# First pairs of a fused attention and gated unit: transposes without casts, attention outputs in single PSUM banks, and w_out exchanged by a permutation matmul

## The chip, the cores and the metric

The kernel runs on one core of one Trainium2 chip. Times are microseconds (us) of one execution on the device. A run that takes over 1.5% more than the fastest of the same kernel is marked slow; ratios use fast runs alone. The profile is one traced execution; its span is a little shorter than the run's time (183.2 us of span in an execution of 185.49 us of the kernel before). PE is TensorE (PEld its weight loads), DVE VectorE, ACT ScalarE, POOL GpSimd, SP SyncE. PEclk is the clock that PE was granted, as a share of full speed.

## The reference

Attention with a causal window, then a gated linear unit with a causal convolution of 5 taps. q, k and v are (8 batches, 8 heads, 576 positions, 64), in fp32. Heads 0 to 3 see the last 32 positions, heads 4 to 7 every fourth one of the last 128.

```python
scores = scale * np.matmul(q, k.transpose(0, 1, 3, 2))
mask_plain = (rel >= 0) & (rel < window)
mask_dil = (rel >= 0) & (rel < window * dilation) & (rel % dilation == 0)
...
x = attn_out.transpose(0, 2, 1, 3).reshape(B, S, H * D)      # (8, 576, 512)
for k in range(K):
    gate_pre += conv_w[k][None, None, :] * xp[:, k:k + S, :]
gate = 1.0 / (1.0 + np.exp(-gate_pre))
return gate * (x @ w_val) @ w_out
```

## The kernel before

Two heads make a pair; there are 32 pairs, numbered 0 to 31. Two pairs make a group, which is one load of q and k, and four pairs make a batch. Two of the four residues of the positions are held with their two heads exchanged, so they need w_val and w_out with the 64-row halves exchanged: `w_val_s` and `w_out_s`. The second was made by a copy from SBUF to SBUF through the DMA engines:

```python
def swap_out():
    for h in range(2):
        nc.gpsimd.dma_start(out=w_out_s[D * h:D * h + D], in_=w_out_b[D - D * h:2 * D - D * h])

def out_tile(G, n):                       # output projection of one half G
    w = w_out_b if G == 0 else w_out_s
    ps = bank()                           # one of 4 single PSUM banks
    ...                                   # 4 matmuls of 512 columns
    osb = out_pool.tile([128, Dm], FP32, name="osb")     # 4 buffers
    nc.scalar.mul(out=osb, in_=ps, mul=0.5)
    ...                                   # stores on the SP queue
```

The order of instructions is the program's own. The loop over pairs, cut to what the change touches:

```python
for i in range(NP):
    ...                                   # loads of groups ahead, on the SP queue
    if i + 1 < NP:
        prep_v(i + 1)                     # v to bf16, on POOL
    if i == 2: ...                        # casts of q, k of group 2, on POOL
    if i == 5:
        swap_out()
    scores(i, 0); scores(i, 1)            # PE, then exp on ACT
    run_conv(i - 1)
    apply_mask(i, 0)                      # DVE
    if i > 0: after_x(i - 1)              # transposes of pair i-1's result
    if 1 < i < NCH: next_pair(i)          # transposes of q, k of pair i+1
    apply_mask(i, 1)
    if 0 < i < 3: make_conv_diag(i + 1)   # DVE
    ...
    attn_v(i, 0); attn_v(i, 1)            # into the banks of the scores
    normalize(i)                          # DVE: one reciprocal, one multiply
    if i == 1 or NCH <= i < EARLY: next_pair(i)
    if i == EARLY - 1: trans_main(g + 1, "k")            # i = 6: group 4
    if i == 0: next_pair(0); finish_mask_d()
    elif i >= EARLY - 1 and a == 0 and g + 1 < 2 * B: trans_rest(g + 1)
    ...                                   # value matmuls, output projections
```

`trans_rest` transposes the last 64 rows of each head of a group, which come by transfers of their own ("rest rows", `qk_rest`).

The softmax here doesn't subtract the row's maximum and nothing guards it: scores larger than these inputs give would overflow.

## Time and profile before

| what | the kernel before |
| --- | --- |
| time, three runs | 184.03 us (183.78 to 184.43) |
| span of the profiled execution | 183.2 us |
| PE waiting for w_out_s | 5.2 us, once |
| pair 7, pair 8, pair 31 start | 44.0, 53.9, 160.7 us |
| PE at half clock | 9.6 to 16.4 and 50.5 to 57.4 us |

The profiled execution (185.49 us) was somewhat longer than these three. Two more are needed for the comparison. The first is the page's chain of the work that ended last, by engine; the second a stretch of the early pairs: its length, then busy us (and instructions) of PE, PEld, DVE, ACT and POOL, PEclk, DMA share and GB/s.

```profile
PE 72%; DVE 7%; POOL 6%; DMA 6%; issue 4%; ACT 2%; POOLq 0%; ACTq 0%
```

```profile
20.00:30.00 10.00, 7.75 (x154) 5.22 (x153) 7.00 (x16) 6.53 (x15) 4.61 (x7) 1.00 1.16 262
```

DMA holds 6% of the chain, and that is the one copy of w_out. In the early stretch no engine is full; only the DMA share is.

### The profile page before, as it was taken

To read this page: it belongs to the slowest core of one execution; us is meant where nothing else is said; L and a number is where in the kernel's file an instruction comes from. 1 tells how busy PE (TensorE), PEld (TensorE's weight loads), DVE (VectorE), ACT (ScalarE), POOL (GpSimd) and SP (SyncE) were. 2 spreads that over 40 slices of the span, in tenths; PEclk is the share of its full clock that TensorE was granted. 3 is DMA by queue.
4 is the path that set the end of the run, shared out by engine and by line. 5 is a ranking of instruction groups with operands and counts; after the bars stand their busy time and mean duration, and the time that the engine had idled before them with its cause. 6 is when DMAs were issued, how large, how long until landed. Compare 5 with 4: busy or idle time off the path is not lost.

```text
span 183.2 us, 6768 instructions
## 1 busy us (share of the span) xinstructions
PE 158.7 (87%) x2799; PEld 108.8 (59%) x2827; DVE 120.2 (66%) x292; ACT 115.9 (63%) x217; POOL 59.2 (32%) x118
## 2 busy tenths in 40 slices
PE   6768878979259999999996999999999999999990
PEld 2445556656137667667774776777677767665540
DVE  4647667855404988688775766976797869773320
ACT  3625764759227677777874788778877786564440
POOL 7857166065302730850093028300750400000000
PEclk9957999999957999999999999999999999999999
DMA  5999999999999999999999999999999322224354
GB/s 149 249 300 326 236 263 260 357 197 193 206 338 245 214 319 362 231 334 334 291 222 300 296 291 221 307 309 290 185 333 343 106 61 61 61 57 106 104 166 145
DMA packets 51688, 42.91 MB, mean 234 GB/s; under 512 B 6997, under 2 KB 46917, under 8 KB 51658
## 3 DMA queue, kind: packets, MB, share of 16 engines
q1 hardware_dynamic: 49888, 40.57, 84.1%
q0 software_dynamic: 1216, 1.57, 4.9%
q8 instruction: 22, 0.36, 0.9%
q10 hardware_dynamic: 554, 0.34, 0.6%
q14 instruction: 8, 0.07, 0.1%
HBM read 33.56 MB, written 9.44 MB: 235 GB/s over the span
## 4 chain that ended last, share of the span: by engine, by line
PE 72%; DVE 7%; POOL 6%; DMA 6%; issue 4%; ACT 2%; POOLq 0%; ACTq 0%
PE ps_bank L599 17%; PE ps_bank L583 14%; PE ps_bank L566 12%; PE ps_bank L365 7%; DMA w_out_s<-w_out_b 6%; PE ps_sc L479 5%; PE ps_sc L436 3%; PE ps_sc L493 3%; PE ps_sc L453 3%; DVE et L465 3%; PE ps_bank L520 3%; PE ps_bank L533 2%; DVE xn L508 2%; PE ps_bank L527 2%; DVE xT L535 1%
## 5 line engine op out<-in xcount | busy, mean ns | idle before, releaser
L456 ACT ACTIVATE et<-ps_sc 128x576 bf16<-128x576 f32 x64 | 38.5, 648 | 13.8 <-PE ps_sc L436 9.9
L604 ACT ACTIVATE osb<-ps_bank 128x512 f32<-128x512 f32 x36 | 21.9, 608 | 32.7 <-PE ps_bank L599 26.1
L589 DVE SCALAR_TENSOR_TENSOR y<-gate,ps_bank 128x288 bf16<-128x288 bf16 x64 | 28.3, 450 | 11.8 <-PE ps_bank L583 9.6
L508 DVE TENSOR_TENSOR xn<-ps_sc,rec 96x768 bf16<-96x768 f32 (+1 forms) x32 | 30.6, 955 | 1.1
L566 PE MATMUL ps_bank<-xT,conv_diag 64*64 64x288 bf16 (+1 forms) x768 | 27.9, 270 | 0.0
L193 POOL CAST k_b<-k_nat 128x512 bf16<-128x512 f32 x14 | 9.2, 679 | 53.9 <-DMA k_nat<-in_k_dram 18.5
L465 DVE TENSOR_TENSOR et<-et,mask_p 128x576 bf16<-128x576 bf16 x32 | 17.4, 547 | 10.8 <-ACT et L456 10.8
L575 ACT ACTIVATE gate<-ps_bank 128x288 bf16<-128x288 f32 x64 | 23.0, 422 | 2.0 <-PE ps_bank L566 1.7
L599 PE MATMUL ps_bank<-w_out_s,y 128*128 128x512 bf16 x59 | 18.4, 394 | 6.1 <-DMA w_out_s<-w_out_b 5.2
L599 PEld LDWEIGHTS <-y 128*128 128x128 bf16 x144 | 12.8, 99 | 17.3 <-issue 6.6
L566 PEld LDWEIGHTS <-conv_diag 64*64 64x64 bf16 x768 | 19.3, 108 | 3.0 <-DVE qB L420 1.0
L583 PE MATMUL ps_bank<-xT,w_val_s 128*128 128x288 bf16 x128 | 20.7, 285 | 0.0
L583 PE MATMUL ps_bank<-xT,w_val_b 128*128 128x288 bf16 x128 | 19.9, 286 | 0.4 <-DVE xT L535 0.4
L465 DVE TENSOR_TENSOR et<-et,mask_d 128x576 bf16<-128x576 bf16 x32 | 15.5, 486 | 6.6 <-ACT et L456 6.4
L535 DVE COPY xT<-ps_bank 128x576 bf16<-128x576 bf16 x32 | 14.6, 456 | 7.4 <-PE ps_bank L533 4.4
L200 POOL CAST vP<-vPst 128x768 bf16<-128x768 f32 x16 | 13.1, 841 | 18.5 <-DMA vPst<-in_v_dram 16.7
L599 PE MATMUL ps_bank<-w_out_b,y 128*128 128x512 bf16 x58 | 17.7, 379 | 0.7
L503 DVE RECIPROCAL rec<-ps_sc 96x12 f32<-96x12 f32 (+1 forms) x32 | 7.4, 231 | 13.8 <-PE ps_sc L479 11.1
L583 PEld LDWEIGHTS <-w_val_s 128*128 128x128 bf16 x128 | 12.1, 97 | 5.6
L479 PE MATMUL ps_sc<-vP,et 64*128 64x65 bf16 x384 | 10.2, 197 | 5.4 <-POOL vP L200 2.9
L479 PEld LDWEIGHTS <-et 64*128 64x128 bf16 x384 | 7.7, 98 | 12.0 <-issue 5.7
L583 PEld LDWEIGHTS <-w_val_b 128*128 128x128 bf16 x128 | 11.7, 98 | 3.6 <-issue 0.2
(93 smaller groups left out, 239.2 us busy)
## 6 DMA issues: line engine op xcount, KB each, us to landing
k_nat<-in_k_dram SPq DMA_DIRECT2D x12, 512.0 KB, 6.5
q_nat<-in_q_dram SPq DMA_DIRECT2D x12, 512.0 KB, 8.0
vPst<-in_v_dram SPq DMA_DIRECT2D x12, 384.0 KB, 8.4
v_st<-in_v_dram SPq DMA_DIRECT2D x6, 512.0 KB, 6.4
k_nat<-in_k_dram SPq DMA_DIRECT2D x8, 256.0 KB, 4.5
out_dram<-osb SPq DMA_DIRECT2D x8, 256.0 KB, 6.4
q_nat<-in_q_dram SPq DMA_DIRECT2D x7, 256.0 KB, 5.0
out_dram<-osb SPq DMA_DIRECT2D x8, 224.0 KB, 5.2
```

The costliest lines, as they stand in the source:

```text
L200: nc.gpsimd.tensor_copy(vPs[b % NVP][:, a:e, :, 0:D], vPst[b % NVP][:, a * NB // 2:e * NB // 2, :].rearrange("p (h u) (j d) -> p h (u j) d ...
L456: nc.scalar.activation(out=e3, in_=ps[:, :, 0:HB], func=AF.Exp, scale=scale)
L465: nc.vector.tensor_tensor(out=e3, in0=e3, in1=m, op=ALU.mult)
L479: nc.tensor.matmul(out=ps[:, z, x * AVS:x * AVS + D + 1], lhsT=et[D * z:D * z + D, h2, col:col + 128], rhs=vPs[b % NVP][D * z:D * z + D, a ...
L508: nc.vector.tensor_tensor(out=dst, in0=av[:, :, :, 0:D], in1=rec[0:R, :, :, None].to_broadcast([R, 2, 6, D]), op=ALU.mult)
L535: nc.vector.tensor_copy(xTs[b % NXT][:, c, :, 2:], pr)
L566: nc.tensor.matmul(out=pss[G][D * hp:D * hp + D, o * T:(o + n) * T], lhsT=conv_diag[D * h:D * h + D, c, K - 1 - m, :], rhs=xt[D * h:D * h ...
L575: nc.scalar.activation(out=gate, in_=pss[G][:, 0:HB], func=AF.Tanh, scale=0.5)
L583: nc.tensor.matmul(out=ps[:, 0:HB], lhsT=w[:, mc, c * 128:(c + 1) * 128], rhs=xt[:, mc, 2 * G:2 * G + 2, 2:], start=(mc == 0), stop=(mc == ...
L589: nc.vector.scalar_tensor_tensor(out=y_half[G][:, c, b * HB:(b + 1) * HB], in0=gates.pop((b, c, G)), scalar=1.0, in1=ps[:, 0:HB], op0=ALU. ...
L599: nc.tensor.matmul(out=ps, lhsT=y_half[G][:, c, 128 * n:128 * n + 128], rhs=w[:, c, :], start=(c == 0), stop=(c == NCH - 1),)
L604: nc.scalar.mul(out=osb, in_=ps, mul=0.5)
```

## The change

The intent has two parts. (a) `w_out_s` comes from a matmul with an identity whose halves are exchanged, so the copy goes. (b) The first pairs are to start faster: q and k of groups 0 and 2 are transposed without a cast first, the transposes of the next pair go ahead of the attention output, and this output gets single banks instead of the scores' banks, so that the next scores need not wait for it. Output projections start at pair 6. The core of the diff (cuts marked):

```diff
-    def swap_out():
-        for h in range(2):
-            nc.gpsimd.dma_start(out=w_out_s[D * h:D * h + D], in_=w_out_b[D - D * h:2 * D - D * h])
+    def swap_out(m, eng):
+        ps = bank()
+        nc.tensor.matmul(out=ps, lhsT=ident_x, rhs=w_out_b[:, m, :], start=True, stop=True)
+        if eng is nc.scalar:
+            nc.scalar.copy(out=w_out_s[:, m, :], in_=ps)
+        else:
+            eng.tensor_copy(w_out_s[:, m, :], ps)
 ... trans_main
-                if not dil:
+                if not dil and g < 4:
+                    for h in range(2):
+                        nc.tensor.transpose(
+                            out=ps[D * h:D * h + D, z, TM * m:TM * m + TM],
+                            in_=hi_bf16(t[name][:, 2 * z + h, D * m:D * m + D]), identity=ident)
+                    continue
+                elif not dil:
 ... attn_v
-        et, ps = st[(i, "et")], st[(i, 1)]
+        if i >= EARLY_AV:                                  # EARLY_AV = 5
+            ps = [st[(i, 1)][:, f, :] for f in range(2)]
+        else:
+            if hf == 0:
+                st[(i, "av")] = [bank(), bank()]
+            ps = st[(i, "av")]
 ... normalize, for i < 5
+        for f in range(2):
+            av = st[(i, "av")][f][0:R, 0:6 * AVS].rearrange("p (x e) -> p x e", x=6)
+            nc.vector.reciprocal(out=rec[0:R, f, :], in_=av[:, :, D])
+            nc.vector.tensor_tensor(...)
 ... the loop
-        if i == 5:
-            swap_out()
-        if 1 < i < NCH:
+        if i < NCH:
             next_pair(i)
-        if 0 < i < 3:
-            make_conv_diag(i + 1)
+        if 0 < i < NCH:
+            make_conv_diag(i - 1)
+        if i == 6:
+            swap_out(0, nc.scalar)
+            swap_out(1, nc.scalar)
         normalize(i)
+        if i == 6:
+            swap_out(2, nc.scalar)
+            swap_out(3, nc.vector)
-            if outs:
+            if outs and i > 5:
                 run_out()
```

The order of POOL's work (v, masks, casts) is rearranged too, and in each of the first pairs one of the dummy matmuls on the tile `junk` (`warm`) is dropped.

More of the change, by code (lines that the diff above doesn't have):

```diff
@@ L55 @@
     NP = B * NCH
+    EARLY_AV = 5
     consts = ctx.enter_context(tc.tile_pool(name="consts", bufs=1))
@@ L74 @@
     ident = consts.tile([128, 128], BF16, name="ident")
+    ident_x = consts.tile([128, 128], BF16, name="ident_x")
     perm = consts.tile([96, 96], BF16, name="perm")
@@ L142, in load_rest, with load_v_half @@
                             ap=[[2 * D, 2 * TR], [S * D, 4], [1, 2 * D]]))
+    def load_v_half(g, z, a, e, eng):
+        b, per = g // 2, NB // 2
+        first, dst = a * per, vPst[b % NVP]
+        if b == 0 and a == 0 and z == 0:
+            eng.dma_start(
+                out=dst[16:D, 0, :],
+                in_=v[0, 0, 0:96, :].rearrange("(p j) d -> p (j d)", j=2))
+            first = 1
+        eng.dma_start(
+            out=dst[D * z:D * z + D, first:e * per, :],
+            in_=bass.AP(
+                tensor=v.tensor,
+                offset=v.offset + (b * H * S + 192 * first + 96 * z - 32) * D,
+                ap=[[2 * D, D], [192 * D, e * per - first], [1, 2 * D]]))
     def load_v(g, a=0, e=4, eng=nc.sync):
@@ L147, in load_v @@
         if not dil:
-            per = NB // 2
-            dst = vPst[b % NVP]
             for z in range(2):
-                first = a * per
-                if b == 0 and a == 0 and z == 0:
-                    eng.dma_start(
-                        out=dst[16:D, 0, :],
-                        in_=v[0, 0, 0:96, :].rearrange("(p j) d -> p (j d)", j=2))
-                    first = 1
-                eng.dma_start(
-                    out=dst[D * z:D * z + D, first:e * per, :],
-                    in_=bass.AP(
-                        tensor=v.tensor,
-                        offset=v.offset + (b * H * S + 192 * first + 96 * z - 32) * D,
-                        ap=[[2 * D, D], [192 * D, e * per - first], [1, 2 * D]]))
+                load_v_half(g, z, a, e, eng)
         else:
@@ L181, in load_group, with cast @@
         load_v(g)
-    def cast(g, name, a, eng):
+    def cast(g, name):
         t = grp_tiles[g]
-        if name + "b" not in t:
-            t[name + "b"] = qb_pool.tile([128, DIL, 4, D], BF16, name=f"{name}_b")
-        dst = t[name + "b"][:, :, a:a + 2, :]
-        src = t[name][:, a:a + 2, :].rearrange("p h (r d) -> p r h d", r=DIL)
-        if eng is nc.scalar:
-            nc.scalar.copy(out=dst, in_=src)
-        else:
-            eng.tensor_copy(dst, src)
+        t[name + "b"] = qb_pool.tile([128, DIL, 4, D], BF16, name=f"{name}_b")
+        for a in (0, 2):
+            nc.gpsimd.tensor_copy(
+                t[name + "b"][:, :, a:a + 2, :],
+                t[name][:, a:a + 2, :].rearrange("p h (r d) -> p r h d", r=DIL))
     def prep_v(i):
@@ L246 @@
     nc.vector.tensor_tensor(out=ident_h, in0=ident[:, 0:D], in1=ident[:, D:2 * D], op=ALU.add)
+    for h in range(2):
+        nc.vector.tensor_copy(ident_x[:, D * h:D * h + D], ident[:, D - D * h:2 * D - D * h])
     nc.gpsimd.memset(ident5, 0.0)
@@ L360, in trans_main @@
             for m in range(4):
-                if not dil:
+                if not dil and g < 4:
+                    for h in range(2):
+                        nc.tensor.transpose(
[3 more added lines that the diff above has]
+                elif not dil:
                     src = t[name + "b"][:, m, 2 * z:2 * z + 2, :]
@@ L373, in trans_main @@
                 dst = t["qT"][:, z0:z1, :, 0:TM]
-                if g == 0:
+                if g <= 2 and len(pairs) == 1:
                     nc.vector.tensor_copy(dst, rt)
@@ L469, in attn_v @@
         b, c, dil, g, a = pair_info(i)
-        et, ps = st[(i, "et")], st[(i, 1)]
+        et = st[(i, "et")]
+        if i >= EARLY_AV:
[4 more added lines that the diff above has]
+            ps = st[(i, "av")]
         if not dil:
@@ L479, in attn_v @@
                             nc.tensor.matmul(
-                                out=ps[:, z, x * AVS:x * AVS + D + 1],
+                                out=ps[z][:, x * AVS:x * AVS + D + 1],
                                 lhsT=et[D * z:D * z + D, h2, col:col + 128],
@@ L493, in attn_v @@
                 nc.tensor.matmul(
-                    out=ps[:, hf, x * AVS:x * AVS + D + 1], lhsT=et[:, hf, col:col + 128],
+                    out=ps[hf][:, x * AVS:x * AVS + D + 1], lhsT=et[:, hf, col:col + 128],
                     rhs=rhs, start=True, stop=True)
@@ L500, in normalize @@
         xn = st[(i, "xn")] = xn_pool.tile([128, 2, 3, 2, D], BF16, name="xn")
-        av = st[(i, 1)][0:R, :, 0:6 * AVS].rearrange("p f (x e) -> p f x e", x=6)
         rec = rec_pool.tile([128, 2, 6], FP32, name="rec")
-        nc.vector.reciprocal(out=rec[0:R], in_=av[:, :, :, D])
         if dil:
@@ L507, in normalize @@
             dst = xn[0:R].rearrange("p z n h d -> p z (n h) d")
-        nc.vector.tensor_tensor(
-            out=dst, in0=av[:, :, :, 0:D],
-            in1=rec[0:R, :, :, None].to_broadcast([R, 2, 6, D]), op=ALU.mult)
+        if i >= EARLY_AV:
+            av = st[(i, 1)][0:R, :, 0:6 * AVS].rearrange("p f (x e) -> p f x e", x=6)
+            nc.vector.reciprocal(out=rec[0:R], in_=av[:, :, :, D])
+            nc.vector.tensor_tensor(
+                out=dst, in0=av[:, :, :, 0:D],
+                in1=rec[0:R, :, :, None].to_broadcast([R, 2, 6, D]), op=ALU.mult)
+            return
+        for f in range(2):
+            av = st[(i, "av")][f][0:R, 0:6 * AVS].rearrange("p (x e) -> p x e", x=6)
+            nc.vector.reciprocal(out=rec[0:R, f, :], in_=av[:, :, D])
+            nc.vector.tensor_tensor(
+                out=dst[:, f], in0=av[:, :, 0:D],
+                in1=rec[0:R, f, :, None].to_broadcast([R, 6, D]), op=ALU.mult)
     def trans_x(i):
@@ L661 @@
     warm(8)
-    cast(0, "k", 0, nc.vector)
-    cast(0, "q", 0, nc.scalar)
     next_pair(-1)
-    setup_conv_w()
-    make_conv_diag(0)
-    make_conv_diag(1)
-    make_mask_d()
-    make_perm()
-    prep_v(0)
     for i in range(NP):
@@ L683 @@
             load_group(g + 3)
-        if i + 1 < NP:
-            prep_v(i + 1)
-        if i == 1:
+        if i == 0:
+            prep_v(0)
+            make_mask_d()
+            prep_v(1)
+            make_perm()
+        elif i == 1:
+            prep_v(2)
             load_weight(w_val_b, moe_w_val)
-        if i == 2:
-            for name in ("k", "q"):
-                cast(2, name, 0, nc.gpsimd)
-        if i == 3:
+        elif i == 2:
+            prep_v(3)
+        elif i == 3:
             load_weight(w_out_b, moe_w_out)
-            for name in ("k", "q"):
-                cast(2, name, 2, nc.gpsimd)
-        if i == 4:
+            prep_v(4)
+        elif i == 4:
             swap_val()
-        if i == 5:
-            swap_out()
-        g2 = g + 2
-        if 2 < g2 < 2 * B and g2 % 2 == 0:
-            cast(g2, "k" if a == 0 else "q", 0, nc.gpsimd)
-            cast(g2, "k" if a == 0 else "q", 2, nc.gpsimd)
+            prep_v(5)
+            prep_v(6)
+        elif i == 5:
+            prep_v(7)
+            cast(4, "k")
+        elif i == 6:
+            cast(4, "q")
+        else:
+            if i < NP - 1:
+                prep_v(i + 1)
+            if g + 2 < 2 * B and g % 2 == 0:
+                cast(g + 2, "k" if a == 0 else "q")
         scores(i, 0)
@@ L705 @@
         if i == 0:
-            cast(0, "k", 2, nc.scalar)
-            cast(0, "q", 2, nc.scalar)
+            setup_conv_w()
         run_conv(i - 1)
@@ L716 @@
         apply_mask(i, 1)
-        if 0 < i < 3:
-            make_conv_diag(i + 1)
+        if 0 < i < NCH:
+            make_conv_diag(i - 1)
         if i < NCH:
-            warm(3 if i == 0 else 2)
+            warm(2 if i == 0 else 1)
         elif c == 0 and outs:
             run_out()
-        elif vals:
+        elif i > NCH and vals:
             run_val()
@@ L726 @@
         attn_v(i, 1)
+        if i == 6:
+            swap_out(0, nc.scalar)
+            swap_out(1, nc.scalar)
         normalize(i)
-        if i == 1 or NCH <= i < EARLY:
+        if i == 6:
+            swap_out(2, nc.scalar)
+            swap_out(3, nc.vector)
+        if i == 0:
+            finish_mask_d()
+        elif i == NCH - 1:
+            make_conv_diag(i)
+        if NCH <= i < EARLY:
             next_pair(i)
@@ L731 @@
             trans_main(g + 1, "k")
-        if i == 0:
-            next_pair(0)
-            finish_mask_d()
-        elif i >= EARLY - 1 and a == 0 and g + 1 < 2 * B:
+        elif i >= EARLY and a == 0 and g + 1 < 2 * B:
+            trans_rest(g + 1)
+        if i == EARLY - 1:
             trans_rest(g + 1)
         if i < NCH - 1:
-            warm(2)
+            warm(1)
         if c == 0 and vals:
```

## The prediction

> **What bounds the kernel now.** I read the page first, then the waits of TensorE (PE), then the chain of waits, the timeline of the first 60 us, and a table of windows. There are 32 pairs of heads, numbered 0 to 31; a group is two pairs (one load of q and k), and four pairs are one batch.
>
> The page: busy shares, then the span in 40 slices of 4.6 us.
>
> ```profile
> PE 158.7 (87%) x2799; PEld 108.8 (59%) x2827; DVE 120.2 (66%) x292; ACT 115.9 (63%) x217; POOL 59.2 (32%) x118
> ...
> PE   6768878979259999999996999999999999999990
> ...
> PEclk9957999999957999999999999999999999999999
> DMA  5999999999999999999999999999999322224354
> GB/s 149 249 300 326 236 263 260 357 197 193 206 338 245 214 319 362 231 334 334 291 222 300 296 291 221 307 309 290 185 333 343 106 61 61 61 57 106 104 166 145
> ```
>
> PE is the busy engine, at 9 tenths from slice 12 (55 us) on with one exception. Its holes are in slices 0 to 11, above all the "25" at 46 to 55 us. The DMA row is full from slice 1 to slice 30: the loads run without a pause until about 142 us. So two things can bound the first 55 us: PE, or the arrival of the loads.
>
> The waits of PE in the first 56 us (total, times, longest):
>
> ```profile
> PE ps_bank L599 <- DMA w_out_s<-w_out_b: 5.2, 1, 5.2
> PE ps_sc L479 <- POOL vP L200: 2.9, 1, 2.9
> ...
> PE ps_sc L493 <- POOL vA L205: 1.3, 1, 1.3
> ...
> PE ps_bank L400 <- DMA qk_rest<-in_q_dram: 0.4, 1, 0.4
> ```
>
> The first is the largest: the output projection of the exchanged half waits for w_out_s, an SBUF to SBUF copy. The second is pair 0 waiting for its v; the third is pair 6. The last is small, yet decides how I read the change, as said below.
>
> The chain of waits around the large one (start, length):
>
> ```profile
> 40.59 0.48 POOL w_out_s L346
> 41.06 10.91 DMA w_out_s<-w_out_b
> 52.11 0.58 PE ps_bank L599
> ```
>
> And the timeline of PE there:
>
> ```profile
> 42.48 0.23 PE L400 MATMUL ps_bank<-ident,qk_rest 128*128 128x128 bf16 x1 [0.39 <-DMA qk_rest<-in_q_dram]
> ...
> 43.99 0.28 PE L453 MATMUL ps_sc<-qA,kA 64*128 64x128 bf16 x4
> ...
> 46.69 0.22 PE L493 MATMUL ps_sc<-vB,et 128*128 128x65 bf16 x2
> ...
> 52.11 0.58 PE L599 MATMUL ps_bank<-w_out_s,y 128*128 128x512 bf16 x1 [5.19 <-DMA w_out_s<-w_out_b]
> ```
>
> Pair 7 starts at 43.99, its last attention matmul ends at 46.9, then PE stands until 52.1. At 42.48, the end of pair 6, PE waited for the transfer of the rest rows of group 4: there it had caught up with the loads. The windows (busy by engine, clock, DMA share, GB/s):
>
> ```profile
> 35.00:40.00 5.00, 3.93 (x63) 2.71 (x65) 3.97 (x9) 3.60 (x8) 1.81 (x3) 1.00 1.19 249
> 40.00:45.00 5.00, 4.21 (x73) 3.04 (x73) 2.33 (x7) 3.47 (x7) 3.65 (x8) 1.00 1.17 194
> 45.00:50.00 5.00, 1.91 (x38) 1.59 (x30) 2.85 (x6) 2.09 (x4) 1.60 (x2) 1.00 1.10 200
> 50.00:55.00 5.00, 2.67 (x41) 1.48 (x46) 0.00 (x0) 0.99 (x2) 0.00 (x0) 0.55 1.11 330
> ```
>
> The DMA share is over 1 all the time, and the clock is halved after the stall: the trace's clock records put it at 0.5 from 50.5 to 57.4 us.
>
> **What the Trainium skill says.** "TensorE: Matmul & The Clock Gate", section "Part 1: The HAM clock gate": PE's clock falls to half after about 3.4 us of idleness and returns after about as long a busy window. The trace agrees: the halved stretch is 6.8 us, two such windows, and begins 3.6 us after PE stopped. It is also halved from 9.6 to 16.4 us. "DMA: Bandwidth & Descriptors", section "Issuing engines are not separate DMA queues" and its rules: transfers of all issuers share the same 16 engines, so a second queue gives no bandwidth. The trace agrees: while w_out_s moves (44 to 51 us) the rate is about 200 GB/s, against 330 just after it. The same page, "Where 436 GB/s comes from", lets an SBUF to SBUF copy be bound by the fabric alone; here 512 KB took 10.9 us, queued among loads. "PSUM — Partial Sum Buffer", "PSUM bank collisions raise a hardware error": what matters between engines is the bank. The change gives each half of an early pair's attention output a bank of its own; no trace line of before prices that.
>
> **The change part by part.**
>
> (a) w_out_s by matmul. Removes the 10.9 us copy. Adds four matmuls of 512 columns in pair 6 (0.22 us each, from the 0.86 us that four such take late in the chain: 0.9 us) and four evacuations (three on ACT at 0.60, one on DVE), before the wait for group 4's rest rows, where PE has time. PE's stall of 5.2 us goes, and so does the cause of its cold clock.
>
> (b) The early pairs: no casts of q and k before the transposes of groups 0 and 2 (0.43 us on DVE, 0.62 on ACT, 0.6 on POOL each), v of pair 0 prepared ahead of mask_d (POOL made mask_d from 6.9 to 9.4 and v at 10.03), next pair's transposes ahead of the attention output, outputs outside the scores' banks. On PE 8 transposes of 64 columns replace 4 of 128, some 0.2 us more a tensor. Pairs 0 to 5 should come 2 to 5 us earlier: pair 0's attention output at about 10 us, since q of pair 1, now ahead of it in PE's order, lands at 9.45 by the trace's landings; pair 4's at about 25.2, not 29.7, since its v lands at 24.2 and takes 0.83 on POOL; pair 5's at 29 to 31.5, not 34.1.
>
> (c) But pair 6 ends, in both kernels, with the transposes of group 4's rest rows. These land at 42.4. The order of the loads on the SP queue up to there is the same, their bytes are the same, and DMA was full from 4 us on. So I expect PE to wait there until 42.4 again, and pair 7 to start at about 44 as before. What (b) gains is given back: 0 us at the end, +/- 0.5.
>
> (d) From pair 7 on. Before: 46.9, stall to 52.1, four projection matmuls at half clock, pair 8 at 53.9. After: 46.9, four projection matmuls 0.87, one value group 0.5 (the old order had done it in pair 4), pair 8 at about 48.3. Gain 5.6. Pair 8 took 6.0 us (53.9 to 59.9) against 17.6/4 = 4.4 in steady state: gain about 1.7 from the clock. One output tile that was done in pair 5 now comes later in a full PE: loss 0.87. Sum: 5.6 + 1.7 - 0.87 = 6.4, so 184.0 - 6.4 = 177.6 us.
>
> (e) The clock again. PE now reaches the end of pair 6 early and idles there: by my working it finishes the transposes of pair 7 near 37.5, waits for k of group 4 (lands 38.0, POOL's cast about 1.2) to 39.3, and then to 42.4: some 4.3 us idle in 5. If that halves the clock for 6.8 us, pair 7 and part of pair 8 run at half speed: 4.7 to 6.8 us of them at half cost 2.4 to 3.4. I give it 5 chances in 10, slightly less after its being partly busy there: expected cost about 1.2. That makes 178.8.
>
> **The rivals.**
>
> First, the loads take the stall's place after pair 7. Steady state moves about 5.1 MB a batch (3.9 in, 1.2 out) in 17.6 us, 290 GB/s, close to what full DMA gives here. In before, PE used k of group 5 at 56.5 (landed 50.3), group 5's rest at 58.7 (53.5), group 6's rest at about 67.5 (62.6), k of group 7 at 74.4 (67.4): slack 5 to 7. The copy's 0.5 MB leaves DMA, and 42 to 52 us moved 2.2 MB of which 1.65 were loads; at 290 GB/s they need 5.7 us, so these loads land about 4 us earlier. Slack 9 to 11 against a gain of 6.4: it holds, by 3 us. Were the 4 us not to come, the gain would be cut to about 5 (179).
>
> Second, the early gain carries through: if group 4's rest rows landed earlier too, pair 7 would start at 39 to 41, and the time would be 173 to 175. For it: PE sheds real waits. Against it: the full DMA row from slice 1.
>
> Third, bank pressure: attention outputs now share the four single banks with transposes, convolution and warm-up matmuls, and conv may wait for the normalisation. For pairs under 5 only, so a few tenths, hidden by (c). That would leave the time as the sum says.
>
> Fourth, (e) in full, and later stops such as the 1.7 us at 98 us, which the trace puts down to no releaser, moving about: 180 to 181, inside the 2%.
>
> **Range and chances.** 178.8 us; 8 in 10 between 175.3 and 181.5: the low end is the sum without a cold clock plus some of the second rival, the high end a cold clock in full and an early stop. The 2% border is 180.3. Faster 0.80, within 2% 0.19, slower 0.01.
>
> **What would show it.** Right: no wait for w_out_s; PE waiting near 42.4 us for the rest rows of group 4; pair 7 at 43 to 44.5 and pair 8 at 48 to 51; DMA full to about 137 instead of 142 us; then batches of 17.6 us. Wrong: pair 7 well before 43 (then (c) fails and the gain is larger), PE waits on k or rest rows in pairs 8 to 13 (the first rival), or a stall on a bank in pairs 0 to 4.

## The result, and the profile after

In the first comparison the changed kernel took 179.71 us at the median (177.65 to 182.06, four runs, two of them slow), beside 184.23 (183.78 to 185.45) for the kernel before. The ratio of the fast runs is 0.9665, 95% interval 0.9568 to 0.9763: faster. A ratio here is the mean time of one kernel's fast runs over that of the other's in the same rounds, so it is not quite the ratio of the medians. The profiled execution is the fastest of the four, while that of the kernel before was a long one, so the two profiles lie further apart (7.3 us of span) than the medians (4.5). A second job with five rounds, told as e4 below, gave a smaller gain.

From the page of the changed kernel: the busy line, then the 40 slices (4.4 us each) of PE, PEclk and DMA, and the chain by engine.

```profile
PE 161.4 (92%) x2856; PEld 109.2 (62%) x2856; DVE 122.2 (69%) x306; ACT 113.9 (65%) x215; POOL 56.0 (32%) x112
...
PE   6779986988999999999999999999999999999980
...
PEclk9955798799999999999999999999999999999999
DMA  5999999999999999999999999999999321225344
...
PE 76%; DVE 10%; DMA 5%; ACT 5%; issue 1%; SPq 0%; DVEq 0%; ACTq 0%
```

PE's row has lost its hole at 46 to 55 us and is full from slice 10 on. DMA is full to about 136 us (31 slices of 4.4), where it was full to 142. But the first ten slices of PE look no better than before, and PEclk has a new dip at slices 6 and 7. DVE's part of the chain rose.

PE's waits in the changed kernel (total us, times, longest); the first is the wait for `junk` at the start, which the kernel before has too:

```profile
PE ps_bank L669 <- DVE junk L239: 1.6, 1, 1.6
PE ps_bank L499 <- DVE et L478: 1.1, 2, 0.7
PE ps_bank L370 <- DMA q_nat<-in_q_dram: 1.1, 1, 1.1
PE ps_bank L370 <- DMA k_nat<-in_k_dram: 0.9, 1, 0.9
```

The wait for w_out_s is gone, and so are those for v on POOL (2.9 and 1.3). In their place PE waits for q and k themselves and for DVE's masking of `et`. No row names the rest rows.

The windows of the changed kernel around the old stall:

```profile
40.00:45.00 5.00, 4.45 (x48) 2.70 (x48) 3.15 (x9) 4.07 (x8) 1.17 (x2) 1.00 1.19 200
45.00:50.00 5.00, 4.89 (x118) 3.64 (x112) 3.88 (x8) 3.83 (x8) 1.82 (x2) 1.00 1.11 334
50.00:55.00 5.00, 5.00 (x114) 3.35 (x102) 3.59 (x10) 4.04 (x9) 1.04 (x2) 1.00 1.19 272
```

PE is busy 4.9 and 5.0 us where it had 1.9 and 2.7, with a full clock. At 45 to 50 us DMA moves 334 GB/s, not 200 (338 in e1, where the copy's going is the only change): without the copy the loads have it. At 40 to 45 the rate is the same in both kernels (200 and 194), so that low rate was not the copy's.

PE's timeline at the end of pair 6 of the changed kernel (start, length, line, operation, out<-in):

```profile
40.52 1.02 PE L349 MATMUL ps_bank<-w_out_b,ident_x 128*128 128x512 bf16 x4
...
42.54 0.61 PE L378 MATMUL ps_bank<-ident,k_b 128*128 128x128 bf16 x8
42.99 0.28 PE L413 MATMUL ps_bank<-ident,qk_rest 128*128 128x128 bf16 x2
...
44.70 0.29 PE L466 MATMUL ps_sc<-qA,kA 64*128 64x128 bf16 x4
```

The rest rows of group 4 landed at 41.9 by the trace and are used at 42.99 without a wait. Pair 7 starts at 44.7, which is 0.7 us later than before. Pair 8 starts at 49.2 (53.9 before), pair 9 at 53.7 (59.9), pair 16 at 84.6 (90.6), pair 31 at 153.1 (160.7). So pair 7 took 4.5 us instead of 9.9, which after its late start leaves 4.7 us; 1.5 more are won in pair 8, and then the distance holds. The further 1.6 at pair 31 come mostly from one step, from pair 17 to pair 18, which took 6.5 us in the profiled execution before (95.1 to 101.6) and 4.5 in that after; e8, the kernel before with more output buffers, had no such step (4.6).

Why the early pairs did not come earlier is read from three views of the changed kernel. First, PE's timeline at pair 0: the transposes of the next pair's q now stand ahead of the attention output (L499), and they wait.

```profile
10.03 0.64 PE L370 MATMUL ps_bank<-ident,q_nat 128*64 128x128 bf16 x8 [1.11 <-DMA q_nat<-in_q_dram]
10.60 1.04 PE L669 MATMUL ps_bank<-junk 128*128 128x512 bf16 x2
11.57 0.94 PE L499 MATMUL ps_bank<-vP,et 64*128 64x65 bf16 x24
```

Pair 0's attention output starts at 11.6 us; before, at 10.9. Second, the windows: the early pairs, and two stretches of 3.4 us each around the clock's new dip.

```profile
20.00:30.00 10.00, 7.29 (x172) 5.19 (x171) 9.00 (x23) 5.89 (x14) 3.16 (x3) 0.99 1.17 239
```

```profile
26.40:29.80 3.40, 1.67 (x44) 1.12 (x45) 3.23 (x8) 1.58 (x4) 1.86 (x2) 1.00 1.18 243
29.80:33.20 3.40, 3.40 (x38) 2.22 (x38) 2.19 (x6) 0.58 (x1) 0.83 (x1) 0.50 1.12 319
```

DVE is busy 9.0 of 10 us, where it was 7.0, and PE works half of 26.4 to 29.8 only; after this its clock is halved for 3.4 us. Third, DVE's own timeline there shows what fills it:

```profile
25.26 1.11 DVE L336 TENSOR_TENSOR conv_diag<-ident_h,conv_w_sb 128x320 bf16<-128x320 bf16 x1
...
26.99 0.18 DVE L535 RECIPROCAL rec<-ps_bank 128x6 f32<-128x6 f32 x1
27.21 0.56 DVE L536 TENSOR_TENSOR xn<-ps_bank,rec 128x384 bf16<-128x384 f32 x1
27.68 0.92 DVE L336 TENSOR_TENSOR conv_diag<-ident_h,conv_w_sb 128x320 bf16<-128x320 bf16 x1
28.52 0.44 DVE L478 TENSOR_TENSOR et<-et,mask_p 128x576 bf16<-128x576 bf16 x1
```

The diagonals of the convolution (before, two of the four were made at the start; now all are made in pairs 1 to 3) took 1.11 and 0.92 us here, and the normalisation comes in two halves of 0.74. The mask on which PE's attention output waits (L478) comes after them. Pair 4's attention output starts at 29.0 (29.7 before), pair 5's at 35.1 (34.1).

DVE is not the whole of it. In this execution the first halved clock lasted from 9.3 to 19.6 us, 3.4 us longer than before. In the profiles of e2, e4, e6 and e10, which have the same early pairs and a halved stretch of 6.8 us there, pair 4 started at 23.1 to 24.0 (25.7 here, 26.5 before), so 2.5 to 3.4 us were won up to it; pair 5 started at 31.5 to 32.1 in all four (32.2 before), so the gain was lost within pair 4. The loads of pair 5 are one more limit there. POOL, without its casts, now reaches the load of w_out at 18.9 us instead of 25.1; pair 5's q lands at 28.8 instead of 26.4 and its v at 30.8 instead of 28.1. PE waited for this q in e2, e9 and e10 (0.4, 0.9 and 1.3 us). No run held the load of w_out back, so what its place costs is not shown.

So the theory: (a) is the whole gain, through the stall, its cold clock and the DMA time of the copy; (b) gives about nothing at the end. Two rivals: that (b) carries a part of it, which the loads then hide or not; and that it is enough to move the copy out of PE's way.

### The profile page after: what moved, and what is told of

It is laid out like the page before. It is cut to its first block, busy times and chain, and to the rows that moved or that the text cites. A ratio compares the mean times of both kernels' runs of the same rounds, so it can differ in the third digit from the quotient of the medians.

```text
span 175.9 us, 6850 instructions
## 1 busy us (share of the span) xinstructions
PE 161.4 (92%) x2856; PEld 109.2 (62%) x2856; DVE 122.2 (69%) x306; ACT 113.9 (65%) x215; POOL 56.0 (32%) x112
## 4 chain that ended last, share of the span: by engine, by line
PE 76%; DVE 10%; DMA 5%; ACT 5%; issue 1%; SPq 0%; DVEq 0%; ACTq 0%
PE ps_bank L627 18%; PE ps_bank L611 17%; PE ps_bank L594 12%; PE ps_bank L378 6%; DMA q_nat<-in_q_dram 5%; DVE et L478 4%; PE ps_sc L499 4%; PE ps_sc L466 3%; PE ps_sc L513 3%; PE ps_sc L449 3%; DVE xT L563 2%; PE ps_bank L548 2%; PE ps_bank L561 2%; ACT et L469 2%; PE ps_bank L555 2%; PE ps_bank L370 1%
## 5 line engine op out<-in xcount | busy, mean ns | idle before, releaser
L529 DVE TENSOR_TENSOR xn<-ps_sc,rec 128x768 bf16<-128x768 f32 (+1 forms) x27 | 25.8, 955 | 0.9
L603 ACT ACTIVATE gate<-ps_bank 128x288 bf16<-128x288 f32 x64 | 23.1, 423 | 2.0 <-PE ps_bank L594 2.0
L192 POOL CAST k_b<-k_nat 128x512 bf16<-128x512 f32 x12 | 7.8, 680 | 43.8 <-DMA k_nat<-in_k_dram 33.7
L611 PE MATMUL ps_bank<-xT,w_val_b 128*128 128x288 bf16 x128 | 20.7, 296 | 0.2 <-DVE xT L563 0.2
L201 POOL CAST vP<-vPst 128x768 bf16<-128x768 f32 x16 | 13.7, 875 | 22.6 <-DMA vPst<-in_v_dram 12.8
L478 DVE TENSOR_TENSOR et<-et,mask_d 128x576 bf16<-128x576 bf16 x32 | 15.9, 496 | 6.5 <-ACT et L469 6.3
L627 PE MATMUL ps_bank<-w_out_b,y 128*128 128x512 bf16 x72 | 18.4, 379 | 0.0
L478 DVE TENSOR_TENSOR et<-et,mask_p 128x576 bf16<-128x576 bf16 x32 | 15.8, 494 | 3.5 <-ACT et L469 3.5
L206 POOL CAST vA<-v_st 128x512 bf16<-128x512 f32 x16 | 10.4, 653 | 12.1 <-DMA v_st<-in_v_dram 12.1
L499 PEld LDWEIGHTS <-et 64*128 64x128 bf16 x384 | 7.8, 99 | 7.7 <-DVE et L478 3.2
L393 ACT COPY kT<-ps_bank 128x1024 bf16<-128x1024 bf16 (+1 forms) x10 | 8.6, 860 | 5.1 <-PE ps_bank L370 5.1
```

The costliest lines, as they stand in the source:

```text
L201: nc.gpsimd.tensor_copy(vPs[b % NVP][:, a:e, :, 0:D], vPst[b % NVP][:, a * NB // 2:e * NB // 2, :].rearrange("p (h u) (j d) -> p h (u j) d ...
L478: nc.vector.tensor_tensor(out=e3, in0=e3, in1=m, op=ALU.mult)
L499: nc.tensor.matmul(out=ps[z][:, x * AVS:x * AVS + D + 1], lhsT=et[D * z:D * z + D, h2, col:col + 128], rhs=vPs[b % NVP][D * z:D * z + D, a ...
L529: nc.vector.tensor_tensor(out=dst, in0=av[:, :, :, 0:D], in1=rec[0:R, :, :, None].to_broadcast([R, 2, 6, D]), op=ALU.mult)
L603: nc.scalar.activation(out=gate, in_=pss[G][:, 0:HB], func=AF.Tanh, scale=0.5)
L611: nc.tensor.matmul(out=ps[:, 0:HB], lhsT=w[:, mc, c * 128:(c + 1) * 128], rhs=xt[:, mc, 2 * G:2 * G + 2, 2:], start=(mc == 0), stop=(mc == ...
```

## The experiments

All twelve runs gave correct results. "Before" is the kernel before in the same job. Pair starts are from the profiled execution, which is one of the runs.

| run | kernel | median (range) us | before | ratio (interval) | pairs 5, 7, 8 start |
| --- | --- | --- | --- | --- | --- |
| e1 | before + (a) | 178.68 (176.99–180.23) | 182.44 | 0.976 (0.970–0.982) | 32.0, 44.8, 49.0 |
| e2 | after − (a) | 182.86 (181.34–186.52) | 182.44 | 1.000 (0.994–1.006) | 32.1, 44.3, 48.5 |
| e3 | before, copy one pair earlier | 180.29 (179.98–180.73) | 182.44 | 0.988 (0.983–0.993) | 31.9, 46.5, 51.1 |
| e4 | after again | 180.21 (178.30–182.05) | 182.44 | 0.985 (0.979–0.991) | 31.7, 43.3, 47.5 |
| e5 | e1, 7 output buffers | 178.27 (177.71–179.95) | 183.07 | 0.981 (0.975–0.987) | 32.0, 45.4, 49.2 |
| e6 | after, 7 output buffers | 177.88 (177.15–180.24) | 183.07 | 0.977 (0.972–0.981) | 31.6, 43.5, 47.7 |
| e7 | after, diagonals on GpSimd | 179.94 (177.74–181.85) | 183.07 | 0.985 (0.978–0.992) | 28.8, 45.5, 51.0 |
| e8 | before, 7 output buffers | 183.81 (182.72–184.71) | 183.07 | 1.009 (1.003–1.016) | 31.7, 44.9, 54.1 |
| e9 | e6 + e7, rest rows first | 176.44 (176.06–179.12) | 183.14 | 0.964 (0.959–0.969) | 33.3, 46.2, 50.4 |
| e10 | e6, rest rows first | 176.90 (176.36–178.28) | 183.14 | 0.967 (0.962–0.972) | 31.5, 44.1, 48.5 |
| e11 | e6 again | 178.28 (176.49–180.81) | 182.67 | 0.975 (0.967–0.983) | 32.1, 44.2, 48.8 |
| e12 | e9 again | 175.88 (175.27–176.61) | 182.67 | 0.965 (0.960–0.969) | 32.6, 43.9, 48.1 |

Jobs, on four chips: e1 to e4; e5 to e8; e9 and e10; e11 and e12. The profiled executions of e1, e2 and e9 were slow ones. The gains of 1 to 2.5% below are read from the intervals, which hold within one job; between jobs there is more (e4).

### e1: part (a) alone

```diff
 (in the kernel before)
-        if i == 5:
-            swap_out()
+        if i == 6: swap_out(0, nc.scalar); swap_out(1, nc.scalar)     # ahead of normalize
+        if i == 6: swap_out(2, nc.scalar); swap_out(3, nc.vector)     # after it
```

> The kernel before with part (a) alone: w_out_s by four matmuls at the end of pair 6. My theory (the copy's stall is the whole gain, the early parts give nothing at the end): about 178 to 180 us, the same as the changed kernel within 1%, pair 8 at 48 to 50 us. Rival (the early parts give part of the gain): 181 to 183 us, clearly slower than the changed kernel.

It is 2.4% faster, and pair 8 starts at 49.0 as in the whole change, though PE's waits for v (2.9 and 1.3 us) are still there. The whole change, e4 in the same job, is not better (0.985; the intervals overlap).

### e2: everything but part (a)

```diff
 (in the changed kernel; swap_out as before)
         elif i == 5:
             prep_v(7)
             cast(4, "k")
+            swap_out()
-        (the four swap_out calls of pair 6)
```

> The changed kernel with the copy by DMA put back (issued at about 39 us as before). My theory: 183 to 185 us, as the kernel before, with a wait for w_out_s of 4 to 6 us and the clock halved after it. Rival (the early parts give part of the gain): 180 to 182 us.

The time is that of the kernel before, as my theory had it, but not by the wait that I expected: with output projections starting at pair 6, the first use of w_out_s comes in pair 8, and the copy had landed by 50.6. Pair 8 starts at 48.5. The profiled execution was a slow one, and lost its lead later, at pairs 20 to 23. There, ACT had no output buffer free, since the stores of the earlier ones had not landed, and PE waited for the bank that ACT was to empty (ACT's and PE's waits in e2):

```profile
ACT osb L628 <- DMA out_dram<-osb: 13.4, 6, 4.3
...
PE ps_bank L551 <- ACT osb L628: 2.7, 1, 2.7
```

Since no fast execution of e2 was profiled, where those lost the same amount is open. What follows is that (b) without (a) gains nothing, and that avoiding the stall while keeping the copy isn't enough.

### e3: the copy one pair earlier

```diff
 (in the kernel before)
             swap_val()
-        if i == 5:
             swap_out()
```

> The kernel before with the same copy issued as soon as w_out_b has landed, about 34 us and not 40.5. If only its lateness costs: no wait for w_out_s, about 178 us. If its share of the DMA engines costs: loads of group 4 land about 3 to 4 us later (rest rows at 45 to 46, not 42.4), pair 7 starts at about 47, and 180.5 to 182 us.

Half the gain, with no wait for w_out_s. The copy now lies among the loads of group 4, whose rest rows land at 43.6, and PE's clock is halved from 41.0 to 47.8. PE's timeline of e3:

```profile
43.27 0.64 PE L400 MATMUL ps_bank<-ident,qk_rest 128*128 128x128 bf16 x2 [0.80 <-DMA qk_rest<-in_k_dram]
...
45.41 1.17 PE L583 MATMUL ps_bank<-xT,w_val_s 128*128 128x288 bf16 x4
```

The four value matmuls at 45.41 took 1.17 us; at full clock (at 48.96 in the same trace) 0.65. So the copy cost in two ways: its lateness, and its share of the DMA engines, by which the rest rows landed 1.2 us later than before. The matmul takes away both costs. That the halved clock is the copy's doing is not shown: it began at 41.0, ahead of the wait for the rest rows, and after a wait of 1.5 us for v (1.3 in the kernel before).

### e4: the whole change again

No edit.

> The changed kernel again. Its first four runs spread from 177.65 to 182.06 us. If the spread is the clock's phase, this profile shows cold stretches at other times and a span that follows them; if it is stalls that come and go in the later batches, the cold stretches are alike and the difference lies after 50 us.

The ratio is 0.985 (0.979 to 0.991), where the first comparison had 0.967 (0.957 to 0.976): the same two kernels in another job, and intervals that don't meet. The kernel before was at 182.4 here and at 184.2 there. So "faster" in the first comparison was not repeated, and ratios of different jobs are compared with care. The ten runs of the two jobs spread from 177.65 to 182.06. The profiled one here (178.30) has pair 8 at 47.5, 1.7 us ahead of the first profile, and pair 31 at 153.8, 0.7 us behind it: it lost 2.4 us in between. Of my two alternatives the second fits better: the halved stretches do lie elsewhere (7.7 to 14.5 and 28.1 to 31.6), but they are 3.4 us shorter in all while the run is longer, and what was lost came after 50 us. ACT waited for output buffers in both, 3.6 us in the first profile and 6.0 in this one. That suggested the next runs.

### e5, e6 and e8: seven output buffers in e1, after and before

```diff
-    out_pool = ctx.enter_context(tc.tile_pool(name="osb", bufs=4))
+    out_pool = ctx.enter_context(tc.tile_pool(name="osb", bufs=7))
```

> The copy replaced by the matmuls alone (as the first experiment), with seven output buffers in place of four. Theory: from about 60 us on the evacuation of the projection waits for stores that queue behind the loads, and with four buffers this blocks PE now and then. Then: fewer or no waits of ACT's output copy for the stores (5.7 us in the first experiment), about 176 to 177 us and a narrower spread. Rival (the stores hide behind other work, the spread is something else): 178 to 179 us and the same spread.

> The changed kernel with seven output buffers. By the store theory 176 to 178 us and a narrower spread than 178.3 to 182.05; if the early parts of the change then cost nothing, equal to the run of the matmul alone with seven buffers within 0.5%; if they cost, up to 1% slower. Rival: no change, about 180 us.

> The kernel before with seven output buffers. Its stall for w_out_s puts the loads ahead, and its trace shows no wait for stores, so the store theory says at most 0.5% off: 182 to 184 us.

ACT's waits before an output buffer's write, in the changed kernel with 4 buffers, and then in e6 with 7:

```profile
ACT osb L632 <- PE ps_bank L627: 17.3, 21, 1.7
ACT osb L632 <- DMA out_dram<-osb: 3.6, 3, 1.5
```

```profile
ACT osb L632 <- PE ps_bank L627: 23.6, 26, 1.7
```

The wait for the stores (out_dram) has gone; ACT waits for PE's matmuls instead, as an engine with time to spare does.

e5 missed: 178.27 us is the rival's range, and its spread (177.71 to 179.95) is not much narrower than that of e1. e6 fell in the range of the store theory. e5 and e6 agree within their intervals (0.981 and 0.977): with the stores out of the way, what (b) adds to (a) is about half a per cent in the means (1.0 us), within the noise: with 4 buffers e4 was 1.6 us slower than e1 in the means of the fast runs. The kernel before doesn't gain from the buffers (1.009). e6 was narrow but for one run; its repeat e11 had three slow runs of six. So the buffers take away a wait, but that they take away the spread is not shown.

### e7: the diagonals on GpSimd

This tests what holds the early pairs, and then what holds pair 7.

```diff
     def make_conv_diag(c):
-        nc.vector.tensor_tensor(
+        nc.gpsimd.tensor_tensor(
 (and called for c = 0 in pair 1, 1 in pair 2, 2 and 3 in pair 3, ahead of the scores)
```

> The changed kernel with its four convolution diagonals made on GpSimd, which is idle from 20 to 25 us, and not on VectorE, busy 9.0 of the 10 us from 20 to 30 there. If VectorE bounds pairs 3 to 5: pair 5 starts near 30 to 31.5 us and not 33.3. If the loads bound the end of pair 6 (my step c): pair 7 still starts at 43 to 44.5, with a wait for the rest rows of group 4 in sight, and the time is unchanged within 0.7 us. If they don't: pair 7 at 41 to 42.5, and 1 to 2 us off the end.

Pair 5 starts at 28.8 (33.3 in the first profile of the change, 31.6 in e6) and pair 6 at 34.4 (37.7 and 36.3). But more than DVE's work differs in this execution: PE's clock was not halved at all before 41.7, so that the eight value matmuls ahead of pair 5 took 1.15 us instead of 2.08, and pair 5's q landed at 27.4 instead of 28.8. e9 and e12 have the same diagonals, and there the clock was halved in pairs 4 and 5, and pair 5 started at 33.3 and 32.6. PE's timeline of e12 in pair 4 has a stop without a releaser and a wait for the mask, though DVE was busy only 7.0 of the 10 us from 20 to 30:

```profile
27.71 0.22 PE L558 MATMUL ps_bank<-perm,xn 96*128 96x96 bf16 x1 [1.50 <-issue]
...
29.07 0.57 PE L502 MATMUL ps_bank<-vP,et 64*128 64x65 bf16 x14 [0.66 <-DVE et L481]
```

So PE's waits for DVE are seen in the changed kernel, but that relieving DVE is enough to bring pair 5 forward is not shown. In e7 itself, what was won by pair 6 is given back at the loads. PE's timeline of e7 (pair 5's attention output, then the rest rows), and its windows:

```profile
32.16 0.55 PE L499 MATMUL ps_sc<-vP,et 64*128 64x65 bf16 x24 [1.40 <-POOL vP L201]
...
42.15 0.29 PE L413 MATMUL ps_bank<-ident,qk_rest 128*128 128x128 bf16 x1 [2.08 <-DMA qk_rest<-in_k_dram]
```

```profile
40.00:45.00 5.00, 2.75 (x11) 1.23 (x10) 0.55 (x3) 1.79 (x4) 1.17 (x2) 0.67 1.21 181
45.00:50.00 5.00, 5.00 (x71) 3.66 (x70) 2.34 (x6) 3.15 (x6) 1.84 (x2) 0.65 1.11 326
```

PE stood 2.1 us for the rest rows of group 4 and ran at half clock from 41.7 to 48.5, and pair 8 came at 51.0, later than in the plain change. An early part that is 3 to 4 us faster made this execution (179.4 us) no faster.

### e9 and e10: the rest rows of group 4 ahead of its q rows

PE needs k and the rest rows of group 4 in pair 6 and q in pair 7 only, yet q was loaded second.

```diff
     def load_group(g):
-        for name in ("k", "q"):
-            load_main(g, name, 0, 4, nc.sync)
+        load_main(g, "k", 0, 4, nc.sync)
+        if g > 4:
+            load_main(g, "q", 0, 4, nc.sync)
         for name in ("k", "q"):
             load_rest(g, name, nc.sync)
+        if g == 4:
+            load_main(g, "q", 0, 4, nc.sync)
 (e9: with 7 output buffers and e7's edit; e10: with 7 output buffers)
```

> The changed kernel with 7 output buffers, the convolution diagonals on GpSimd (as in e7) and, for group 4 alone, the rest rows loaded ahead of the main q rows. My theory, that the arrival of group 4 is what takes back the early gain: the rest rows land at about 39.5 to 40.5 instead of 42.56, PE's wait for qk_rest of 2.1 us falls under 0.5, pair 7 starts at 42.5 to 44 (45.5 in e7), and the time is 176 to 177.5, 1 to 2 us under the kernel with 7 buffers alone (177.9). The rival, that PE meets the loads wherever they end: the wait moves to the q rows of group 4 in pair 7 or to the rows of group 5, pair 8 starts at 47.5 to 51, and the time stays at 177.5 to 179.

> The changed kernel with 7 output buffers and the rest rows of group 4 ahead of its main q rows; the convolution diagonals stay on VectorE. Here PE hardly waited for the rest rows, so both theories say no change: pair 7 at 43 to 44.5, pair 8 at 47 to 49, time 177.3 to 178.5. If it is faster by over 1 us, pair 6 was bound by that load after all and I misread its chain.

e9 took 176.44 us, in the range of my theory. Its profile, of a slow execution, has no wait for the rest rows, but pair 7 at 46.2, not the 42.5 to 44 expected. e10 took 176.90, level with e9 in the same job, so the diagonals on GpSimd add nothing that shows. For it both theories had said no change from the 177.88 of e6, and 177.3 at the least: a miss. It is explained if e6 is bound by this load in some of its executions. The trace of e6 makes that likely and doesn't show it: group 4's rest rows landed at 41.72 and PE used them at 41.82, 0.1 us later, so an execution with PE any earlier would wait, as e2's did (1.2 us). In e10 the rest rows were there in time, and PE met the loads earlier instead, at pair 5's q (PE's timeline of e10):

```profile
28.94 0.64 PE L373 MATMUL ps_bank<-ident,q_nat 128*64 128x128 bf16 x8 [1.29 <-DMA q_nat<-in_q_dram]
```

Pair 4 had started at 23.1 there (24.0 in e6, 25.7 in the first profile of the change), yet pair 5 started at 31.5. PE's clock was halved from 28.2 to 35.0.

### e11 and e12: e6 and e9 side by side

No new edit.

> The changed kernel with 7 output buffers once more (e6 over), as the neighbour on the same chip of the next run. If the earlier rest rows were worth about 1 us, this run is at 177.4 to 178.2 and 0.8 to 1.8 us above the next; if the difference between e6 and e9 was only one of chips, the two agree within 0.5 us.

> e9 once more: 7 output buffers, diagonals on GpSimd, rest rows of group 4 ahead of its q rows; its first profile fell on its slowest execution. By my theory 176 to 177 with pair 7 at 42 to 44.5 and no wait over 0.5 us for qk_rest; if it is level with its neighbour (177.4 to 178.2), the earlier rest rows gave nothing and e9's 176.4 was the chip.

e12 took 175.88 us (all six fast), e11 178.28 (three of six slow). Over fast runs only, the means are 175.9 and 176.9. So the version of e9 is the best found, by about 1 us over e6 in fast runs (the two intervals overlap, and leaving out e11's slow runs makes the difference smaller), at 0.964 and 0.965 of the kernel before, where the change as given had 0.967 and 0.985. In its profile PE uses the rest rows of group 4 at 42.17, without a wait, and pair 7 still starts at 43.9, since PE itself was late (pair 5 at 32.6). The profile thus doesn't show where the 1 us lies.

## Why the prediction was right or wrong

**The time, 178.8: right.** The first comparison gave 179.71 and the second 180.21, both in the range of 175.3 to 181.5. The ratio, 0.967 and 0.985, lies on both sides of the 2% border; e1, e5 and e6, which hold part (a) as well, lie at 0.976 to 0.981. That 178.8 is so near has some luck in it: the 1.2 us of it that (e) brought in, for a halved clock at 38 to 45, did not come there, and the fastest run (177.65) is at the sum without them.

**(a), right, and it is the whole gain.** e1 alone has it and e2 without it has none; a part of 1 us or so for (b) would not show in these runs. The four matmuls took 1.02 us (0.9 expected), ahead of group 4's rest rows, at a price that doesn't show. My sum had priced the stall and the clock; e3 (no stall, half the gain) and e2 (no stall in its profile, no gain) show that the copy costs more than its stall.

**(b), wrong in what it does early.** "Pairs 0 to 5 should come 2 to 5 us earlier" failed: pair 0's attention output came at 11.6, not 10, pair 4's at 29.0, not 25.2, pair 5's at 35.1, not 29 to 31.5. I had set pair 0's output right behind the landing of q (9.45 in the trace before), but in the changed kernel q landed at 9.99, and its transposes and two matmuls on `junk` came first, 1.6 us. And I had counted PE, POOL and the loads for pairs 2 to 5 but not DVE, to which the change gave the diagonals and the halved normalisation: 9.0 us busy of 10. The halved clock I had counted for pairs 7 and 8 only, and the landings were taken from the trace before, where w_out's load came later. In e2, e4, e6 and e10 the gain was there up to pair 4 and gone at pair 5. e7 doesn't bear out the estimate either: its pair 5 started at 28.8, but its attention output came at 32.2, after 1.4 us of waiting for v, and e9 and e12 started pair 5 at 33.3 and 32.6. The transposes themselves cost next to nothing: eight of 64 columns took 0.42 us, four of 128 took 0.39.

**(c), right in the number; in the profiled execution another limit came first.** I expected PE to wait until 42.4 for the rest rows, with pair 7 at about 44. Pair 7 came at 44.7, but the wait was not there, so in this execution the number is luck: PE itself was late, and the load, landed at 41.9, stood about 1 us behind it. The limit I had named does lie where I put it in other executions: e7 waits 2.1 us for these rows, to 42.15, and e2 1.2 us, to 42.31. "Given back: 0 us, +/- 0.5" is finer than the runs resolve: e6 was 1.0 us faster than e5, and e4 1.6 us slower than e1.

**(d), right.** Pair 8 was expected at 48.3 and came at 49.2, since pair 7 was 0.7 late. The gain there was 4.7 (5.6 expected), and pair 8 itself took 4.5 us against 6.0, so 1.5 for the clock (1.7 expected). By pair 16 the gain was 6.0, the sum having said 6.4. What the profile then shows over it is one stop of the kernel before.

**(e), not in the place I put it in the change, but real.** No halved clock at 38 to 45 in the changed kernel; it came at 29.8 instead, for 3.4 us. In e7, where PE did idle before the rest rows, it came at 41.7 for 6.8 us, the case that I gave 5 chances in 10. The page "TensorE: Matmul & The Clock Gate" of the Trainium skill, section "Part 1: The HAM clock gate", calls the window free-running and its effect variable from run to run. The traces agree as to the effect: the same kernel had 9.3 to 19.6 us at half clock in one profile and 7.7 to 14.5 in another (e4); they don't show the window itself.

**The rivals.** The first (the loads take the stall's place after pair 7) did not come: no wait for k or rest rows in pairs 8 to 13, and the group 5 rows landed at 47.5 to 49.4, not 50.3 to 53.5, about 3 to 4 us earlier, as worked out. The second (the early gain carries through) did not come in the change; with the rest rows first (e9, e12) the kernel gains about 1 us, and whether that is this early gain is not shown. The third, banks, did not show: no wait of PE is put down to the reader of a bank alone, and those for DVE's `xn`, which also frees a bank, were 0.6 and 0.2 us. The fourth, stops that move about, is the one that I had too small: five of the ten runs of the change took over 180 us. The stores that wait behind the loads (3.6 and 6.0 us of ACT's waits) are one such stop; that they make the whole spread is not shown, as e11 was wide with 7 buffers.

## What to carry to other kernels

When a stall of a few us ends in a transfer, ask for its two costs apart, the lateness and the share of the DMA engines: here moving the copy (e3) returned half of what removing it (e1) did. An early part that shares one full stream of loads is worth only what the last load it meets allows, so look at the order in which the next load's pieces are needed before making the compute ahead of it faster. And when a change takes waits away from one engine, add up every other engine in the same 10 us, because the one that got the small jobs may become a bound; and look at several profiles before one is named, for here the clock and the loads moved too.

## What the Trainium skill lacked or had wrong

- "TensorE: Matmul & The Clock Gate", Part 1, gives an idle window as the condition of the half clock, without a busy share that still counts as idle. Here it also came after windows in which PE was busy about half the time: 1.67 of 3.40 us (26.4 to 29.8 in the changed kernel, half clock from 29.8) and 1.84 of 3.40 (5.9 to 9.3, half clock from 9.3).
- "DMA: Bandwidth & Descriptors", "Where 436 GB/s comes from", has the fabric as the bound of a copy from SBUF to SBUF, and no figure for such a copy among loads. Here 512 KB took 10.9 us (about 9 in e3), and all transfers together moved 200 GB/s at 45 to 50 us, against 334 in the same stretch without the copy.
- No page that I read says how stores behind a full stream of loads hold output buffers: ACT waited 3.6 and 6.0 us for stores with 4 buffers (two profiles of the changed kernel), and not at all with 7 (e6).
